# Three real products instead of four for the spectral multiplication, with the last seven frequencies of four units packed together

## The chip, the cores and the metric

The kernel runs on one core of one Trainium2 chip. The metric is device time in microseconds (us): the time of one execution as the device reports it. TensorE (PE) multiplies matrices into PSUM (8 banks of 128 partitions x 512 fp32), VectorE (DVE), ScalarE (ACT) and GpSimd (POOL) work elementwise, SyncE (SP) issues the DMAs.

## What is computed

For each of 4 batch entries, 6272 steps and 256 channels: a gated recurrence, then three projections of its result, a circular convolution over time of the middle one with a given filter, a product of the three, and an output projection.

```python
sig = 1.0 / (1.0 + np.exp(-f_logit))
f = lower_bound + (1.0 - lower_bound) * sig
h = f[:, t] * h + (1.0 - f[:, t]) * x[:, t]        # for each t, giving y
...
proj = y @ w_proj                                  # three blocks of 256: x1, x2, x3
X2 = np.fft.rfft(x2, n=S, axis=1)                  # S = 6272
H = np.fft.rfft(filter_fft, n=S, axis=0)
x2_conv = np.fft.irfft(X2 * H, n=S, axis=1)
out = (x1 * x2_conv * x3) @ w_out
```

The line that the change touches is `X2 * H`: a product of complex numbers for each frequency and channel.

## The kernel before, in words

**Transform.** 6272 is 128 x 49. The Fourier transform is done as two small transforms by matmul: one over 128 (table `D1`), one over 49 (table `FT`, with its inverse in `VA` and `VB`), with the channels as further columns. After the first transform a channel pair holds 64 columns `k`; the second turns the 49 residues into 49 frequencies with a real and an imaginary part: 98 rows (`TB`). Channels are worked in 16 *units* (`NU`) of 8 channel pairs (`UE`); four units (`NA`) form a group whose first transforms lie in the tile `A` at the same time.

**Setup** (`prepare`). It builds the tables (`iotas`, `args0`, `args1`: DVE makes arguments, ACT takes the sine; then table pieces on DVE and POOL), loads the filter, rotates it (`rot`, line 637), and transforms it unit by unit: `FF1` (line 661), copies `afs`, `FF2` (line 679), a copy `hw`, and a store to the DRAM tiles `H`. The spectrum of the filter is stored with some rows twice, so that a load can bring both (real, imaginary) and (imaginary, real) orders to the 98 rows. `last` (line 697) does the column `k = 0` apart. In between, the recurrence of batch entry 0 runs.

**Recurrence** (`hgrn`, 13 chunks of 512 steps): loads, `sig` on ACT (line 337), `u` on POOL (339), `su` transposes on PE (351), `f` on ACT or DVE (364, 366), `scan` on DVE (372), `wrap`, a copy of the first 3072 steps behind the last (303 on POOL, 291 on ACT, or a DMA).

**Each batch entry** then goes through
- `P` (line 725): the middle projection, 98 matmuls, with copies `x2` into the tile `X2`;
- for each group of four units: `F1` (737) and the copy `A` for each unit; `mini` (753) with the product `zm` (761) for the column `k = 0`; then for each unit `H` (load of the filter's spectrum), `F2` (795, eight matmuls of 64 contracted rows, two side by side), the products, `I2` (835, sixteen matmuls back) and the copy `Th`;
- `gate`: `x13` (line 400), copies `xs`, and `z` = x1 * x3, on DVE straight from PSUM (422) or on POOL (431);
- `phase_o`: `I1` (869), `y` on DVE (875), `proj` (887), copy `o`, store.

`y` needs every `z` and `I1` needs every `Th`, so the gate and all units of a batch entry come before its output stage; the recurrence of the next entry is woven into both.

**The products.** A unit's spectrum stands in two PSUM banks (one for each channel of the pairs). For each bank the product with the filter has 2 x 8 x 63 = 1008 elements on 98 rows: (real, imaginary) times two arrangements of the filter. Either DVE does it straight from PSUM (`MUL`, line 816), or ACT or DVE copies the bank to SBUF and POOL multiplies (`pm`, 825). `I2` sums the two halves with `VA` and `VB`.

**Order.** Every operation is numbered as the code is read. `ORDER` is a string with three characters for each operation: its number, its engine and its PSUM bank. `Plan.emit` issues the operations in that order, so it fixes the order on every engine and who does what. The numbers in `op(...)` such as `{"PE": 0.43}` are a planner's costs; they do not act when the kernel runs. PSUM is taken in pairs of banks by most operations, so there are four pairs.

Of the kernel before, what the change touches and what calls it, by code (L numbers as in the profile page):

```python
# [9 lines left out]
F32 = mybir.dt.float32  # L10
# [11 lines left out]
S = 6272  # L22
# [3 lines left out]
TB = 98  # L26
CH = 512
# [14 lines left out]
HP = 128  # L42
HT = 64
# [3 lines left out]
PW = 116  # L47
# [17 lines left out]
class Plan:  # L65

    ROWS = ("su", "F2", "mini", "I1", "FF2", "last")
# [73 lines left out]
    "J4XGluJyYJ2BGsUGgSG1QJ3YGwEGhKGmYHQgJ5WJ6PG5AMrgHGSGtYMsgGkYJ9VJ7uGxYHHCJ+RGusJ8YGpWJ/FHMSGqGG3oGvYG+UG6YHZgKABHIW"
    "HNKG4YGyQHJGHAsHKSGzAG2YHigKBYG7WHLCHCsHBYKCQG/YG8GHORHRTHDYHrgHPJKDVHTDHVrHSYKHXKEAHUYKITKJHKFtKMSHWYMtAHEQKKrKGY"
    "KOKHaWKLYHFAMuYH+gH0UHcuHXSH1EH4QHeuHdYHYCHjUHbYHkYH5AHlsHfYIHgH2WMWYHgSH3GHnsHmYHsQHhCH6WHuoHoYIQgHpUHtYH7GMiYH/S"
    "HwoHvYHqEH8WKNQIBCIIUH9OHxYIZgIDqIRRICYIKEHyWITBKPoIEYKRUHzGIMsKQYKSTIiQIAYKTEIsgILYIFWIjAINYKUrKWVKVYKXTIGGKYNMXQ"
    "KZDIJYIVpI1gISYIaWIUYMYAMbUIeGMZIIWYIOSM3gMcEM4gKbXIPCMdMKaYI+gIXQKdHImSIYAIcuIbYMegMjUIfYInCIkQMkMIdYIoWIlAKcTMlM"
    "KgSMaYJHgIpGItQKerKiCIqUMnWIvoKfYIxAKhTNDgMoGIyYIgRIrMNEgIwYM5AMpOKlQI2UIhBKjrMvWIuYKnAI3YI6sKkYMzSM6YMwGKmQNPgI4E"
    "MxOKqRI7YNQgM0CIzUKsBM1KM7WI5YI0ENFAKrVKooKvTKttKpYM8GM/QNGYKuYKxDJIUM9ONbgNAAI8SNcgJMENBIKwXJKEK0WI9CJLYI/UKyvK2G"
    "K1RJBsKzYNHSK3BNRAK5WJDsJCYJAYK4YNLQNICNlgK7OJEYJFUNMANSYNmgNJKK6WJGEK+XNdANNINKgK/VNTTLAHJJYNeYK8uNXQNUDLBtK9YLDX"
    "NvgNYANVLLEWLCYMygLFHLISNwgLJVLKCNOgLNXJNYLGuLLFNfSNZILHYLPHNiUNgCLOWN6gNnANhKLMYN5gJOQNWgNjENoYLQuRtSJPANkMRuXLRY"
    "RvCLSQRwHLXSLTINxANpUMmYNsWLYKNqENyYLUQODgNtGOEgNrMLZSLVANuOLcULaCLWgNzQLdMRyWN0ALhSR0GN1IN2UN7ALmWONgN3ELiKOOgLeQ"  # L150
    "N8YLbgOFAM+gN4MLjSMqgLfALnOLrULkCOGYN9QLsMOAWN+ALoSOXgOBGN/IOYgM2gOHULpCNagOCOLwQOPAOKSLxILtWUwgOLCOQYLlgOIEOMKLyQ"
    "LuGOJML1SLzAORWL2KL0gRzROSGLqgL6UOZANCAOTOOUSOaYR1BU8gL7MU9gObWL3QOcGOVCOdOOWKOeUL4AL8WVJgVIgOfMUxgMEQL9GOgMLvgL/S"
# [825 lines left out]
```

## Time and profile before

| | |
|---|---|
| device time, median of 3 runs | 460.54 us (460.45 to 461.36) |
| profiled execution: device time | 459.27 us |
| profiled execution: span, first to last instruction | 457.5 us |
| mean granted clock of TensorE | 0.998 |
| `P` of the four entries starts at | 73.8, 169.9, 271.3, 368.9 us |
| last instruction | 457.5 us |

The span leaves out 1.8 us of the profiled execution's time, and that execution lies 1.3 us below the median of the runs. The stages are read by time: setup with the first recurrence to about 74 us, then for each entry a stage `P` of some 11 us, a stage of units and gate, and a stage of output with the rest of the next recurrence; the last entry has no next recurrence. A PE instruction's record reaches to a modelled end, so a busy PE is not a PE at full rate. For the rate one takes pieces of the chain of waits in which matmuls of one kind follow each other, and divides the time by their number.

### The profile page before, as it was taken

How to read it: one execution, taken by the hardware profiler on the slowest of the kernel's cores; microseconds unless marked ns; L12 is line 12 of the kernel's file. 1: busy time of each engine (PE TensorE's matmuls, PEld its weight loads, DVE VectorE, ACT ScalarE, POOL GpSimd, SP SyncE). 2: the span in 40 equal slices, each digit the busy share in tenths (PEclk: the TensorE clock that was granted, in tenths of full speed). 3: DMA queues.
4: the chain of work that ended last, by engine and by line, in shares of the span. 5: the costliest groups of instructions: out<-in, count | busy, mean ns of one | idle time of the engine just before them, and what ended most of it. 6: DMA issues, size and time to landing. Idle time of an engine off the chain costs nothing.

```text
span 457.5 us, 14613 instructions
## 1 busy us (share of the span) xinstructions
PE 443.7 (97%) x6009; PEld 346.2 (76%) x6009; DVE 408.9 (89%) x461; ACT 399.3 (87%) x550; POOL 300.9 (66%) x274
## 2 busy tenths in 40 slices
PE   8998999999999999999999999999999999999995
PEld 6876777767766889777668889767768897677784
DVE  7599996799999993999999986999999977999873
ACT  5989998889999989989998979999989868988563
POOL 4489892289899425778996616989896405976400
PEclk9999999999999999999999999999999999999999
DMA  8999999776979997477779995487969930575176
GB/s 323 407 366 333 357 356 347 284 262 203 313 259 298 326 339 299 179 250 246 241 272 287 350 315 240 142 288 297 308 205 308 351 124 18 192 238 179 48 294 271
DMA packets 46451, 122.59 MB, mean 268 GB/s; under 512 B 4528, under 2 KB 9648, under 8 KB 46384
## 3 DMA queue, kind: packets, MB, share of 16 engines
q1 hardware_dynamic: 46384, 121.65, 75.4%
q8 instruction: 47, 0.77, 0.7%
q14 instruction: 20, 0.16, 0.1%
HBM read 86.12 MB, written 31.98 MB: 258 GB/s over the span
## 4 chain that ended last, share of the span: by engine, by line
PE 70%; DVE 15%; ACT 8%; issue 4%; POOL 2%; DVEq 0%; ACTq 0%; POOLq 0%
PE PS L400 15%; PE PS L725 9%; PE PS L835 8%; PE PS L887 8%; PE PS L351 7%; DVE HA L372 6%; PE PS L737 6%; PE PS L795 6%; DVE ys L875 4%; PE PS L637 3%; PE PS L869 3%; PE PS L661 3%; ACT fTs L364 2%; ACT HA L291 2%; PE PS L603 2%
## 5 line engine op out<-in xcount | busy, mean ns | idle before, releaser
L339 POOL TENSOR_TENSOR XT<-XT,FL 128x1024 f32<-128x1024 f32 (+1 forms) x49 | 110.0, 2247 | 52.1 <-ACT FL L337 28.9
L372 DVE TENSOR_TENSOR_SCAN HA<-fTs,HA,PS 128x512 f16<-128x512 f32 (+1 forms) x96 | 113.2, 1203 | 1.1 <-ACT fTs L364 0.2
L400 PE MATMUL PS<-HA,W 128*128 128x490 f16 (+1 forms) x416 | 102.7, 367 | 1.0 <-DVE HA L372 0.4
L825 POOL TENSOR_TENSOR PP<-HA,Hu 98x1008 f16<-98x1008 f16 x38 | 79.7, 2104 | 5.1 <-ACT HA L291 2.7
L291 ACT CAST HA<-PS 128x1024 f16<-128x1024 f32 (+1 forms) x96 | 78.2, 837 | 5.3 <-PE PS L737 2.9
L431 POOL TENSOR_TENSOR zt<-gx 128x490 f16<-128x490 f32 (+1 forms) x43 | 52.1, 1217 | 45.0 <-DVE ys L875 16.7
L816 DVE TENSOR_TENSOR PP<-PS,Hu 98x1008 f16<-98x1008 f32 x58 | 68.1, 1200 | 0.0
L875 DVE TENSOR_TENSOR ys<-PS,zt 128x1024 fp32r<-128x1024 f32 (+1 forms) x52 | 58.9, 1152 | 7.8 <-PE PS L869 4.7
L887 PE MATMUL PS<-Wo,ys 128*128 128x256 f32 x392 | 58.2, 294 | 1.6 <-DVE ys L875 1.5
L364 ACT ACTIVATE fTs<-PS,cc 128x512 f32<-128x512 f32 (+1 forms) x83 | 54.8, 675 | 5.1 <-PE PS L351 4.3
L400 PEld LDWEIGHTS <-W 128*128 128x128 f16 x416 | 34.6, 97 | 30.4 <-issue 6.8
L835 PEld LDWEIGHTS <-PP 98*128 98x128 f16 x1024 | 49.9, 97 | 9.7 <-issue 1.6
L835 PE MATMUL PS<-VV,PP 98*128 98x98 f16 x1024 | 55.9, 206 | 0.3
L887 PEld LDWEIGHTS PS<-Wo,ys 128*128 128x128 f32 x392 | 49.7, 188 | 6.6 <-DVE ys L875 2.9
L291 ACT CAST Th<-PS 128x784 f16<-128x784 f32 x59 | 48.3, 821 | 6.6 <-PE PS L835 4.6
L293 ACT ACTIVATE gx<-PS 128x490 f32<-128x490 f32 (+1 forms) x84 | 48.3, 584 | 2.5 <-PE PS L400 1.5
L337 ACT ACTIVATE FL<-FL 128x1024 f32<-128x1024 f32 (+1 forms) x49 | 49.4, 1010 | 0.0
L725 PE MATMUL PS<-W,HA 128*128 128x256 f16 x392 | 44.6, 273 | 0.2
L351 PEld LDWEIGHTS PS<-iden,FL 64*128 64x128 f32 x736 | 31.2, 138 | 16.8 <-DVE HA L372 2.9
L725 PEld LDWEIGHTS <-HA 128*128 128x128 f16 x392 | 42.9, 142 | 1.3 <-DVE HA L372 0.3
L351 PE MATMUL PS<-iden,FL 64*128 64x64 f32 x736 | 42.2, 231 | 1.6 <-DVE HA L372 0.8
L291 ACT CAST X<-PS 128x1024 f16<-128x1024 f32 (+1 forms) x31 | 32.6, 1092 | 10.3 <-PE PS L725 9.0
(130 smaller groups left out, 745.6 us busy)
## 6 DMA issues: line engine op xcount, KB each, us to landing
FL<-in_f_logit_dram SPq DMA_DIRECT2D x45, 512.0 KB, 5.5
XT<-in_x_dram SPq DMA_DIRECT2D x45, 512.0 KB, 6.4
Hu<-H SPq DMA_DIRECT2D x39, 512.0 KB, 4.8
out_dram<-osb SPq DMA_DIRECT2D x22, 512.0 KB, 4.6
out_dram<-PP SPq DMA_DIRECT2D x16, 512.0 KB, 5.3
Hx<-H SPq DMA_DIRECT2D x13, 512.0 KB, 4.4
out_dram<-HA SPq DMA_DIRECT2D x10, 512.0 KB, 5.5
X<-in_moe_filter_fft_dram SPq DMA_DIRECT2D x9, 512.0 KB, 7.2
```

Source lines behind the costliest of these rows:

```text
L291: nc.scalar.copy(dst, src)
L339: op("u", {"POOL": 0.1 + 0.553 * nb}, lambda e, xt=xt, ft=ft: nc.gpsimd.tensor_tensor(xt, xt, ft, op=AOP.mult), r=[("ft", k)], w=[("xt", k)])
L351: nc.tensor.transpose(bank(pb)[:, at[p] + j:at[p] + hn:nb], src[ps, j, cols], iden[ps, ps])
L364: nc.scalar.activation(fT, sT, AF.Identity, scale=by, bias=1.0)
L372: nc.vector.tensor_tensor_scan(h, fT, bank(pb)[:, 512 - hn:512 + hn], init, op0=AOP.mult, op1=AOP.add),
L400: nc.tensor.matmul(PS[:, p, 0:n], W13[:, kh, js], HA[:, HB[kh] + t0:HB[kh] + t0 + n], start=(kh == 0), stop=(kh == 1))
L725: nc.tensor.matmul(pp[:, r - r0, :], column(HB[kh], q_of(r)), W2[:, kh, :], start=(kh == 0), stop=(kh == 1))
L816: nc.vector.tensor_tensor(pr, px.unsqueeze(1).broadcast_to([TB, 2, UE, 63]), hh, op=AOP.mult)
L825: nc.gpsimd.tensor_tensor(pr, spec[:, o, :, 1:64].unsqueeze(1).broadcast_to([TB, 2, UE, 63]), hh, op=AOP.mult)
L835: nc.tensor.matmul(PS[:, ib + o, pr * TB:(pr + 1) * TB], PP[:TB, k, o, n, 2 * pr:2 * pr + 2, :], v[:TB], start=(n == 0), stop=(n == 1))
L875: nc.vector.tensor_tensor(late["ys"][:, yk, :, 0:rn * 128], PS[:, cb:cb + 2, 0:rn * 128], late["zt"][:].rearrange("p k r m -> p k (r m)") ...
L887: nc.tensor.matmul(po[:, i, :], late["ys"][:, yk, kh, i * 128:(i + 1) * 128], Wo[:, kh, :], start=(kh == 0), stop=(kh == 1))
```

## The change

The complex product is done with three real products: with X = a + ib and the table rows for a, b and a + b, one multiplies three rows by three rows of the filter's spectrum and lets the inverse table do the sums. Rows per frequency go from 2 to 3, elements per row from 2 to 1. 49 x 3 = 147 rows do not fit 128 partitions, so 42 frequencies (`QM`; 126 rows, `KM`) are done unit by unit, and the last 7 (`QL`; 21 rows) of four units go into four blocks of 32 partitions of one tile. `F2` writes 126 rows with the same eight matmuls; its products have 8 x 63 = 504 elements per bank instead of 1008. New for each group of four units: `FL` (32 matmuls with 32 weight columns each), `slot`, and `pl` on DVE (1008 elements). `mini` has ten matmuls instead of four and `zm` two products. `I2` keeps sixteen matmuls: one of each pair takes the unit's own rows, the other the packed ones with a table that is zero outside the unit's block.

In the setup: `FFL` (8 operations of 8 matmuls) and `hwl` (4 copies) make the packed filter spectrum, which stays in SBUF (`HL`); `last` has 20 matmuls; `args1` and the tables grow; the store of the spectrum is one DMA of 126 rows for each two units instead of two, and a load brings 126 rows of 1024 numbers instead of 128 rows of 2048. `X2` has a pitch of 114 instead of 116. The order is new: 2460 entries instead of 2410.

```diff
-PW = 116
+PW = 114
...
-    FT = konst.tile([128, 2, 2, 128], F16, name="FT")
+    FT = konst.tile([128, 2, 2, 160], F16, name="FT")
+    VM = konst.tile([128, TB], F16, name="VM")
+    VL = konst.tile([128, NA, TB], F16, name="VL")
...
-                        nc.tensor.matmul(PS[:, pb + e2, :], FTr[rows, r, 0:M], af[rows, r],
+                        nc.tensor.matmul(PS[:KM, pb + e2, :], FTm[rows, r], af[rows, r],
...
+                def rest(e, pb, u=u):
+                    for j in (u % NA - 1, u % NA):
+                        for r in range(2):
+                            for e2 in range(2):
+                                rows = slice(64 * e2, 64 * e2 + 64)
+                                at = 96 + 128 * r - 32 * j
+                                nc.tensor.matmul(PS[:, pb + e2, :], FTl[rows, at:at + 128],
+                                                 afs[j % 2][rows, r], start=(j == 0 and r == 0),
+                                                 stop=(j == NA - 1 and r == 1))
+                more = u % NA == NA - 1
+                hl = op("FFL", {"PE": 0.9}, rest, r=[("af", j, h) for j in range(2) for h in range(2)] + FTu,
+                        w=[("FF2L", u // NA)], **(dict(src=fl) if more else dict(take=2)))
...
+                    op("hwl", either(1024), lambda e, pb, q=u // NA: copy(e, HL[q], PS[:, pb:pb + 2], HS),
+                       r=[("FF2L", u // NA)], w=[("HL", u // NA)], src=fl)
...
+    def rest(b, q):
+        k = count["l"] % NP
+        count["l"] += 1
+        def mm(e, xb):
+            for o in range(2):
+                ks = slice(32 * o, 32 * o + 32)
+                for r in range(2):
+                    for j in range(NA):
+                        for e2 in range(2):
+                            rows = slice(64 * e2, 64 * e2 + 64)
+                            nc.tensor.matmul(
+                                PS[32 * j:32 * j + 32, xb + e2, :].rearrange("p (i k) -> p i k", k=64)[:, :, ks],
+                                FT[rows, o, r, 128:160], A[rows, j * UE:(j + 1) * UE, r, ks],
+                                start=(r == 0), stop=(r == 1))
+        fl = op("FL", {"PE": 0.65}, mm, r=[t for i in range(NA) for t in At(i) + Ax(i)] + ["FT0", "FT1"], take=2)
...
+        op("pl", {"DVE": 1.11}, lambda e, xb: nc.vector.tensor_tensor(
+            PP[:, k, 1, :, :, 1:64], blocks(PS[:, xb:xb + 2]), blocks(HL[q]), op=AOP.mult),
+           r=[("HL", q)], w=[("PL", k)], src=fl)
...
-            Hv(h)[:HP].rearrange("p a e k -> p a (e k)"), turned(H[u // 2][u % 2])),
+            Hv(h)[:KM].rearrange("p e k -> p (e k)"), H[u // 2][0:KM, u % 2]),
...
-                            PS[:, xb + e2, :].rearrange("p (i k) -> p i k", k=64)[:, :, ks],
-                            FT[rows, o, r, :], A[rows, ka:ka + UE, r, ks],
+                            PS[:KM, xb + e2, :].rearrange("p (i k) -> p i k", k=64)[:, :, ks],
+                            FT[rows, o, r, 0:KM], A[rows, ka:ka + UE, r, ks],
...
-                    nc.vector.tensor_tensor(
-                        pr, px.unsqueeze(1).broadcast_to([TB, 2, UE, 63]), hh, op=AOP.mult)
+                    nc.vector.tensor_tensor(pr, px, hh, op=AOP.mult)
...
-                    nc.gpsimd.tensor_tensor(
-                        pr, spec[:, o, :, 1:64].unsqueeze(1).broadcast_to([TB, 2, UE, 63]), hh,
-                        op=AOP.mult)
+                    nc.gpsimd.tensor_tensor(pr, spec[:, o, :, 1:64], hh, op=AOP.mult)
...
-                    for n, v in enumerate((VA, VB)):
-                        nc.tensor.matmul(PS[:, ib + o, pr * TB:(pr + 1) * TB],
-                                         PP[:TB, k, o, n, 2 * pr:2 * pr + 2, :], v[:TB],
+                    for n, (a, v) in enumerate(((PP[:KM, k, 0, o], VM[:KM]), (PP[:, kl, 1, o], VL[:, u % NA]))):
+                        nc.tensor.matmul(PS[:, ib + o, pr * TB:(pr + 1) * TB], a[:, 2 * pr:2 * pr + 2, :], v,
                                          start=(n == 0), stop=(n == 1))
```

What the two orders, read entry by entry, give to each engine (operations of a kind, before and after):

| | before | after |
|---|---|---|
| products: DVE straight from PSUM / copy by ACT / copy by DVE (both copies then POOL) | 85 / 41 / 2 | 74 / 45 / 9 |
| `A`: ACT / DVE | 55 / 9 | 48 / 16 |
| `Th`: ACT / DVE | 59 / 5 | 55 / 9 |
| `xs` copies: ACT / DVE | 118 / 29 | 116 / 38 |
| `z`: DVE from PSUM / POOL | 61 / 43 | 54 / 50 |
| `wrap`: ACT / POOL / DMA | 3 / 18 / 27 | 12 / 14 / 22 |
| `afs`: ACT / DVE | 24 / 8 | 20 / 12 |
| new on PE | | 16 `FL`, 8 `FFL` |

On SP, one half of the first chunk's loads of the recurrence now stands ahead of the filter's loads, and ACT's first operation is that chunk's `sig`.

369 lines of the change are left out of this document (210 added, 159 removed).

## Prediction

> **What bounds the kernel now.** I read the page's first part, the windows by stage, the chain of waits for the rate of each kind of matmul, and the groups of instructions by shape. First the page and the windows (window in us, length, then busy time of PE, PEld, DVE, ACT, POOL with instruction counts, clock, DMA share, GB/s):
>
> ```profile
> PE 443.7 (97%) x6009; PEld 346.2 (76%) x6009; DVE 408.9 (89%) x461; ACT 399.3 (87%) x550; POOL 300.9 (66%) x274
> ```
> ```profile
> 0.00:22.00 22.00, 20.62 (x117) 16.92 (x117) 15.21 (x46) 16.49 (x16) 10.52 (x28) 1.00 0.93 364
> 22.00:74.00 52.00, 49.30 (x617) 37.95 (x615) 48.63 (x54) 49.68 (x73) 42.20 (x46) 1.00 0.97 348
> ...
> 85.00:144.00 59.00, 57.66 (x843) 40.25 (x841) 57.12 (x64) 55.75 (x82) 51.17 (x42) 1.00 0.78 255
> 144.00:170.00 26.00, 24.96 (x426) 21.01 (x426) 25.70 (x26) 23.44 (x33) 13.27 (x8) 1.00 0.94 332
> ...
> 382.00:430.00 48.00, 47.91 (x630) 34.40 (x629) 46.02 (x56) 40.91 (x62) 36.21 (x37) 1.00 0.45 146
> ```
>
> PE looks full everywhere, but DVE and ACT are nearly full too: in the units-and-gate stage of entry 0 (85 to 144) DVE 57.12 of 59 us, in the output stage (144 to 170) 25.70 of 26. What PE really needs comes from rates. Pieces of the chain between 12 and 100 us (start, length, what):
>
> ```profile
> 26.88 1.03 PE PS L351 x32
> ...
> 29.25 1.24 PE PS L679 x8
> ...
> 67.03 1.14 PE PS L661 x8
> ...
> 84.64 1.65 PE PS L400 x8
> ...
> 92.35 0.11 PE PS L753 x4
> 92.47 0.44 PE PS L795 x8
> ...
> 94.70 0.75 PE PS L835 x16
> 95.45 0.45 PE PS L737 x8
> ```
>
> So one matmul takes 0.206 us (`x13`), 0.047 (`I2`), 0.055 (`F2`: 0.11 for a side-by-side pair), 0.056 (`F1`), 0.032 (transposes), 0.143 (`FF1`) and 0.155 (`FF2`). Now the matmuls of the stage 85 to 144, and two rows of 382 to 430 (where there are no transposes, and the others are the same 256, 128 and 128):
>
> ```profile
> L400 PE MATMUL PS<-HA,W 128*128 128x490 f16 x83 | 21.0, 370 | 0.2 <-ACT Th L291 0.2
> L835 PE MATMUL PS<-VV,PP 98*128 98x98 f16 x256 | 14.0, 206 | 0.0
> L795 PE MATMUL PS<-HA,FT 64*128 64x256 f16 x128 | 9.5, 271 | 0.0
> L737 PE MATMUL PS<-D,X 128*128 128x128 f16 x128 | 9.5, 219 | 0.5 <-DVE HA L296 0.2 <-ACT HA L291 0.2
> L351 PE MATMUL PS<-iden,FL 64*128 64x64 f32 x112 | 6.3, 232 | 0.0
> L351 PE MATMUL PS<-iden,XT 64*128 64x64 f32 x112 | 5.9, 223 | 0.1
> ```
> ```profile
> L400 PE MATMUL PS<-HA,W 128*128 128x490 f16 x84 | 20.7, 370 | 0.0
> ...
> L400 PE MATMUL PS<-HA,W 128*128 128x392 f16 x8 | 1.5, 328 | 0.0
> ```
>
> Stage 85 to 144: 91 x 0.206 + 256 x 0.047 + 128 x 0.055 + 128 x 0.056 + 224 x 0.032 + 0.45 for `mini` = 52.6 of 59 us: 0.89. (Eight of the 91 are shorter; the sum is an upper one.) Stage 382 to 430: 92 x 0.206 + 12.0 + 7.0 + 7.2 + 0.45 + about 1 for eight projection matmuls = 46.6 of 48 us: 0.97. So with the next recurrence woven in, DVE (0.97) and ACT (0.94) limit, and PE has some 6 us to spare; in the last entry PE itself limits. The clock is 1.00 throughout and plays no part.
>
> **The change part by part.**
>
> *Elementwise work of the entries.* The rows (mean ns of one):
>
> ```profile
> L825 POOL TENSOR_TENSOR PP<-HA,Hu 98x1008 f16<-98x1008 f16 x38 | 79.7, 2104 | 5.1 <-ACT HA L291 2.7 <-DVE zp L761 1.3 <-PE PS L835 0.9
> L816 DVE TENSOR_TENSOR PP<-PS,Hu 98x1008 f16<-98x1008 f32 x58 | 68.1, 1200 | 0.0
> ...
> L291 ACT CAST HA<-PS 128x1024 f16<-128x1024 f32 x55 | 55.2, 1020 | 3.6 <-PE PS L737 2.9 <-issue 0.2
> ...
> L431 POOL TENSOR_TENSOR zt<-gx 128x490 f16<-128x490 f32 x40 | 49.1, 1232 | 43.1 <-DVE ys L875 16.7 <-ACT gx L293 11.4 <-ACT gx L291 9.2
> L291 ACT CAST Th<-PS 128x784 f16<-128x784 f32 x59 | 48.3, 821 | 6.6 <-PE PS L835 4.6 <-DVE gx L296 1.2
> ...
> L422 DVE TENSOR_TENSOR zt<-PS,gx 128x490 f16<-128x490 f32 x56 | 36.4, 656 | 1.1 <-ACT gx L293 0.8
> ...
> L291 ACT CAST HA<-PS 98x512 f16<-98x512 f32 x41 | 23.1, 591 | 1.8 <-PE PS L795 0.9 <-PE PS L753 0.4
> ...
> L296 DVE CAST HA<-PS 128x1024 f16<-128x1024 f32 x9 | 10.9, 1220 | 1.5 <-PE PS L737 1.1 <-POOL PP L825 0.4
> ...
> L296 DVE CAST Th<-PS 128x784 f16<-128x784 f32 x5 | 4.8, 967 | 0.1
> ...
> L296 DVE CAST HA<-PS 98x512 f16<-98x512 f32 x2 | 1.4, 676 | 0.0
> ```
>
> A product of 504 elements on DVE isn't in the trace; the 490-element product of `z`, 0.656 us, is the nearest row, so 0.66 (half of 1.20 would be 0.60). DVE before: 85 x 1.20 = 102.0 (the 58 of the row and 27 that read `Hx`). After: 74 x 0.66 + 16 `pl` x 1.20 = 68.0. Removed: 34.0. But the order gives DVE more copies: `A` 7 x 1.22 + `Th` 4 x 0.97 + copies ahead of POOL 7 x 0.68 + nine `xs` at 0.66 less seven `z` at 0.66 + one `x2` of 1024 elements at 1.22 = 19.7. Net -14.3 us, **-3.6 for each entry**. ACT: -7 x 1.02 - 4 x 0.82 + 4 copies at some 0.6 - 3 others at 0.6 to 1.1, plus five more `wrap` copies at 0.6: about -7, -1.8 for each entry. POOL: 43 x 2.10 = 90.4 (38 and 5 with `Hx`) against 54 x 1.1 (half of 2.10 to the 1.23 of the 490-element row) = 59, and 7 more `z` and 16 small `slot`: -18 in all. POOL is not full (66%); shorter products shorten a unit's way to `I2`, nothing else. The loads of the spectrum carry half as much, but no wait in the stages ends on them, so I count this at nothing.
>
> *PE in the entries.* `F2` and `I2` keep their matmuls and columns: nothing. `FL`: 32 matmuls of 256 columns, eight tiles side by side. Column tiles are not in the trace. If all eight run together as `F2`'s two do: 4 x 0.11 = 0.44 us. If matmuls cannot follow each other closer than the 0.032 of the transposes: 1.0. If only pairs run together: 32 x 0.055 = 1.76. I take 0.75, between the first two, since the starts of a side-by-side pair are what `F2` already shows. `mini` has six matmuls more at 0.03: +0.2. So 4 x 0.95 = **+3.8 us for each entry** (2.6 to 7.8).
>
> The Trainium skill, page "TensorE: Matmul & The Clock Gate", section "Part 3: Packing small matmuls — row/col tiling", states that packed tiles take one matmul's time and about 4 ns for each further tile. By it `FL` would be an estimated 4 x (0.11 + 0.03) = 0.55 us, and the sum 0.8 us less for each entry; no run here shows column tiles yet.
>
> *Where these meet.* Stage 85 to 144: PE 52.6 + 3.8 = 56.4. At the 0.97 that the last entry shows feasible this takes 58.1 us, so the 3.6 that DVE gives can shorten the stage by 0.9 at most unless transposes move behind it. I take **-1 for each of three entries: -3**. Last entry: 46.6 + 3.8 = 50.4, at 0.97 52.0 instead of 48: +4; DVE there is at 46.02 of 48 and gets 3.6 free, which may let PE run a little denser: **+3.5**. The tail behind 430 does not change.
>
> *Setup.* DVE before 22 us: `args1` gets about 20 more column operations and the tables some more:
>
> ```profile
> L293 ACT ACTIVATE Hu<-PS 128x1024 f16<-128x1024 f32 x6 | 6.0, 1024 | 0.6 <-PE PS L679 0.5
> ...
> L545 DVE SCALAR_TENSOR_TENSOR cols<-cols 128x1 f32<-128x1 f32 x1 | 0.2, 160 | 0.0
> ```
>
> 20 x 0.16 = 3.2, and some 2 for wider tables: 15.2 + 5.2 = 20.4 of 22 us busy, so its waits for the rotated filter no longer fit; and half a chunk, 0.5 MB at 364 GB/s = 1.4 us, is loaded ahead of the filter. `FF1` starts later by 1.5 (0 to 3); behind it stand all `afs` and so `FF2`. From 22 to 74: ACT +4 `hwl` x 1.02 and four `wrap`, less one `sig` and the moved copies: +4; DVE +2.8 (four `afs`, one `hw`, two fewer `f`). Both are at 0.94 to 0.96 there, so half of 6.8, 3.4, less 1 for gate work done early: +2.5. PE: eight `FFL` at 1.24 us (eight matmuls of `FF2`) = 9.9, and `FF1` 128 x 0.143 + `FF2` 64 x 0.155 + 392 transposes x 0.032 = 40.8 leave it 11 of 52 us: hidden just about, but each group holds one of four PSUM pairs from its first `FFL` to `hwl`: +1. The stores are halved; DMA share is 0.97 there, yet the waits there end on DMA only for the filter's first loads: nothing. Setup: **+5** (2 to 10).
>
> Sum: 5 - 3 + 3.5 = **+5.5 us**. Against the profiled execution's own 459.27 that is 464.8; the median of the runs shown lies 1.27 above it, so I forecast **466.0** for the median.
>
> **The rivals.**
>
> *DVE decides (ends faster).* Mechanism: between 85 and 170 us DVE is busy 82.8 of 85 us and every other engine less. If `FL` costs 0.44 (PE +2.6) and the order moves half of the stage's transposes (3.6 us) into the output stage, the whole 3.6 that DVE gives comes off each of the three entries: -10. With the last entry at +1 and setup at +2.5: -7, so 453.5. It decides from the point where `FL` costs less than about 0.6 us. For it: DVE at 0.97 to 0.99 in both stages. Against it: ACT at 0.94 gives only 1.8.
>
> *No change.* The same terms in between (entries -2.5 each, last +2.5, setup +5) give 460.5.
>
> *Setup decides.* `FFL` and its held PSUM pair are not hidden: +9.9 instead of +1 on top of the start: setup +10 to 14, in all 471 to 475. Against: the 11 us that PE has there.
>
> *Column tiles do not run together.* `FL` at 1.76: +16 in all, PE over 0.97 in every stage: 466 + 14 = 480. For: nothing in the trace shows more than two tiles together.
>
> *Weight loads become visible.* These rows are the loads of `F2` and of the transposes:
>
> ```profile
> L351 PEld LDWEIGHTS PS<-iden,FL 64*128 64x128 f32 x736 | 31.2, 138 | 16.8 <-DVE HA L372 2.9 <-issue 2.9 <-ACT gx L291 1.5
> ...
> L795 PEld LDWEIGHTS <-FT 64*128 64x128 f16 x512 | 22.0, 96 | 9.9 <-issue 6.5
> ```
>
> `F2`'s weights go from 128 to 126 columns. If its loads took the 138 ns of the transposes' and stood open: 42 ns x 512 = 21 us, 487. Against: the transposes have those loads and still follow each other at 32 ns, and each pair of `F2` streams 110 ns over them. The Trainium skill, same page, section "Weight-path perf modes — Fast Weight Load (FWL) and DoubleRow", says that the fast load needs exactly 128 weights and a type other than fp32, which speaks against this change; the trace agrees in that fp32 loads are longer (138 against 96 ns).
>
> **How the numbers follow.** Forecast (461.5 to 470): 0.40. DVE decides (448 to 459.5): 0.33. No change: 0.08. Setup: 0.09. Column tiles: 0.06. Weight loads: 0.04. A measurement of this kernel tells about 0.2% (0.9 us) from no change. Faster by more: 0.33; within: 0.08; slower: 0.59. The range leaves out the two dearest rivals and the far third of the faster one: 451 to 477. The likeliest case alone is 461.5 to 470.
>
> **What would show it.** Right or wrong are: `FL`'s length in the chain (0.44, 0.75, 1.76); the 504-element product on DVE (0.66) and on POOL (1.1); the start of the first `P` (73.8 before; 79 by the forecast); the length from the first to the second `P` (96 before; 95, and 92.5 if DVE decides); the last entry's stage from `P`'s end to its last `I2` (48 before; 51.5). The forecast is wrong if `FL` lies outside 0.44 to 1.0, if setup grows by less than 2, or if the three middle entries each lose or gain over 3 us.

## The result, and the profile after

The changed kernel takes 483.67 us (median of 4 runs, 483.28 to 485.88) against 460.95 us for the kernel before on the same chip: a ratio of 1.049 (95% interval 1.044 to 1.054). It is slower by 22.7 us, where 5.5 were forecast, and lies outside the range. The profiled execution took 483.28 us with a span of 481.5 us.

The first part of the page of the changed kernel (busy time, share of the span, instructions):

```profile
span 481.5 us, 16035 instructions
...
PE 466.5 (97%) x6693; PEld 365.6 (76%) x6693; DVE 405.4 (84%) x535; ACT 401.8 (83%) x550; POOL 281.1 (58%) x304
```

PE is busy 22.8 us longer than before (443.7), and the span grew by 24.0 us. (Both spans are of the profiled executions; that of the kernel before was 1.7 us faster than its median here and that of the changed kernel 0.4, so the stage differences below add up to 24.0 and not to 22.7.) PE's idle time, span less busy, is 13.8 us before and 15.0 after. DVE's busy time fell by 3.5 us, POOL's by 19.8, and neither shows in the time. The same in the windows of the stages (setup, then units and gate, output, and the last entry's units and gate):

```profile
24.00:81.50 57.50, 54.74 (x654) 41.77 (x652) 50.16 (x52) 52.39 (x73) 41.00 (x46) 1.00 0.85 297
...
93.00:154.00 61.00, 60.04 (x949) 44.86 (x947) 51.68 (x73) 52.92 (x74) 41.61 (x48) 1.00 0.47 150
154.00:182.00 28.00, 27.53 (x470) 22.34 (x468) 27.96 (x26) 26.17 (x40) 17.68 (x10) 1.00 0.88 310
...
399.00:453.00 54.00, 54.00 (x796) 39.27 (x795) 43.04 (x66) 41.20 (x60) 30.16 (x43) 1.00 0.25 81
```

In the units-and-gate stage DVE went from 57.12 of 59 us to 51.68 of 61: the relief arrived, and the stage became longer. Only in the output stage is DVE still full. The stages by the starts of `P` (us):

| | first `P` | entry 0 | entry 1 | entry 2 | entry 3 to the end |
|---|---|---|---|---|---|
| before | 73.7 | 96.1 | 100.4 | 98.6 | 88.7 |
| after | 85.5 | 99.2 | 103.6 | 102.6 | 90.6 |
| difference | +11.8 | +3.1 | +3.2 | +4.0 | +1.9 |

The sum is 24.0. (These are first matmuls on PE's timeline; in the chain of waits of the kernel before the first `P` begins at 73.8 and entry 2's at 271.3, after its first rows at 270.2.) Within an entry, from `P`'s end to the last `I2` takes 2.4, 4.8, 3.9 and 2.3 us longer; the output stages differ by -1.6 to +0.3.

What was added, in the groups by shape of the changed kernel (the new products, then `FL`, `FFL`, `mini`, and the weight load of `F2`):

```profile
L908 DVE TENSOR_TENSOR PP<-PS,Hx 126x504 f16<-126x504 f32 x40 | 26.0, 674 | 2.8 <-PE PS L887 2.2 <-ACT HA L295 0.4
...
L852 DVE TENSOR_TENSOR PP<-PS,Hu 128x1008 f16<-128x1008 f32 x16 | 19.2, 1200 | 0.4 <-PE PS L844 0.4
...
L916 POOL TENSOR_TENSOR PP<-HA,Hf 126x504 f16<-126x504 f16 x30 | 34.0, 1143 | 6.4 <-ACT HA L295 2.7 <-issue 2.4 <-DVE HA L300 1.1
...
L844 PE MATMUL PS<-HA,FT 64*32 64x256 f16 x512 | 10.0, 270 | 0.0
...
L734 PE MATMUL PS<-afs,Hf 64*128 64x512 f32 x32 | 5.6, 426 | 0.0
L734 PE MATMUL PS<-Hx,Hf 64*128 64x512 f32 x32 | 5.0, 388 | 0.0
L813 PE MATMUL PS<-HA,FT 64*126 64x64 f16 x32 | 4.7, 288 | 0.1
L818 PE MATMUL PS<-HA,FT 64*32 64x16 f16 x128 | 3.5, 196 | 0.0
...
L887 PEld LDWEIGHTS <-FT 64*126 64x126 f16 x512 | 27.0, 132 | 9.0 <-issue 7.0
```

And one `mini`, `FL` and the `F2` behind it on PE's timeline (start, length, operation):

```profile
202.75 0.30 PE L813 MATMUL PS<-HA,FT 64*126 64x64 f16 x2
202.98 0.22 PE L818 MATMUL PS<-HA,FT 64*32 64x16 f16 x8
203.02 0.62 PE L844 MATMUL PS<-HA,FT 64*32 64x256 f16 x32
203.56 0.65 PE L887 MATMUL PS<-HA,FT 64*126 64x256 f16 x8
```

`FL` holds PE for 0.54 us here, and 0.57 in the mean of the sixteen. The 270 ns in its group are modelled ends of overlapping matmuls, so what counts is the distance from start to start.

PE's whole timeline can be added up in this way, from each start to the next one, so that a wait counts with the matmul ahead of it. Behind the first `P`, `FL` takes 9.1 us and `mini` 5.0 instead of 1.8: 12.3 us more. All other matmuls there together take 381.9 us, against 382.0 before. Ahead of the first `P`, `FFL` takes 8.8 us, `last` 0.7 more and the matmuls without a use that fill PE's time before `FF1`, with the waits behind them, 2.4 more; the rest together is the same to 0.1 us. So the 24 us are PE's new work, some 21.8 us, and 2.4 us at the start, and nothing that DVE and POOL gave back made the rest of PE's work any shorter.

In the setup DVE's arguments take 9.6 us in one piece (9.05 to 18.6; before 3.96), and the copies of the rotated filter stand behind them on DVE; `FF1` starts at 25.3 instead of 22.2. `FFL` stands in the chain of waits (start, length, what):

```profile
30.26 1.13 PE PS L734 x8
...
44.84 0.99 PE PS L734 x8
...
60.60 1.12 PE PS L734 x8
65.45 0.97 PE PS L734 x6
74.72 1.12 PE PS L734 x8
78.96 1.11 PE PS L734 x7
```

At its end PE stands still inside the first `P`, until two copies on ACT let go (timeline):

```profile
84.61 3.06 ACT L297 ACTIVATE X<-PS 126x512 f16<-126x512 f32 x2
...
85.48 1.04 PE L786 MATMUL PS<-W,HA 128*128 128x256 f16 x8
...
87.72 1.47 PE L786 MATMUL PS<-W,HA 128*128 128x256 f16 x12 [1.20 <-ACT X L297]
```

These are the copies of the column `k = 0`: before it was one of 1.4 us.

### The profile page after: what moved, and what is told of

It is laid out like the page before. It is cut to its first block, busy times and chain, and to the rows that moved or that the text cites. A ratio compares the mean times of both kernels' runs of the same rounds, so it can differ in the third digit from the quotient of the medians.

```text
span 481.5 us, 16035 instructions
## 1 busy us (share of the span) xinstructions
PE 466.5 (97%) x6693; PEld 365.6 (76%) x6693; DVE 405.4 (84%) x535; ACT 401.8 (83%) x550; POOL 281.1 (58%) x304
## 4 chain that ended last, share of the span: by engine, by line
PE 76%; DVE 15%; issue 3%; ACT 3%; POOL 2%; DVEq 0%; POOLq 0%; ACTq 0%
PE PS L404 16%; PE PS L924 9%; PE PS L786 9%; PE PS L355 8%; PE PS L976 7%; PE PS L887 7%; DVE HA L376 6%; PE PS L798 6%; DVE ys L964 5%; PE PS L958 3%; PE PS L697 3%; PE PS L844 2%; PE PS L639 1%; PE PS L715 1%; PE PS L734 1%
## 5 line engine op out<-in xcount | busy, mean ns | idle before, releaser
L404 PE MATMUL PS<-HA,W 128*128 128x490 f16 (+1 forms) x416 | 105.1, 367 | 0.7 <-DVE HA L300 0.6
L435 POOL TENSOR_TENSOR zt<-gx 128x490 f16<-128x490 f32 (+1 forms) x50 | 60.7, 1218 | 66.4 <-DVE gx L300 22.8
L295 ACT CAST HA<-PS 128x1024 f16<-128x1024 f32 (+1 forms) x93 | 72.3, 810 | 14.1 <-PE PS L887 7.3
L924 PEld LDWEIGHTS <-PP 126*128 126x128 f16 (+1 forms) x1024 | 51.2, 98 | 8.9 <-issue 1.5
L924 PE MATMUL PS<-VM,PP 126*128 126x98 f16 x512 | 54.3, 208 | 0.0
L924 PE MATMUL PS<-VL,PP 128*128 128x98 f16 x512 | 54.1, 207 | 0.0
L404 PEld LDWEIGHTS <-W 128*128 128x128 f16 x416 | 33.4, 97 | 26.4 <-issue 6.2
L297 ACT ACTIVATE gx<-PS 128x490 f32<-128x490 f32 (+1 forms) x82 | 46.8, 579 | 8.0 <-PE PS L404 6.1
L295 ACT CAST Th<-PS 128x784 f16<-128x784 f32 x55 | 44.9, 820 | 7.0 <-PE PS L924 5.6
L355 PE MATMUL PS<-iden,XT 64*128 64x64 f32 x736 | 39.4, 223 | 0.2 <-POOL XT L343 0.2
```

The source lines that it names most:

```text
L295: nc.scalar.copy(dst, src)
L355: nc.tensor.transpose(bank(pb)[:, at[p] + j:at[p] + hn:nb], src[ps, j, cols], iden[ps, ps])
L404: nc.tensor.matmul(PS[:, p, 0:n], W13[:, kh, js], HA[:, HB[kh] + t0:HB[kh] + t0 + n], start=(kh == 0), stop=(kh == 1))
L435: nc.gpsimd.tensor_tensor(zd(), xs(0), xs(1), op=AOP.mult)
L924: nc.tensor.matmul(PS[:, ib + o, pr * TB:(pr + 1) * TB], a[:, 2 * pr:2 * pr + 2, :], v, start=(n == 0), stop=(n == 1))
```

## The experiments

Two theories stood against each other. A (in the expectations also "PE theory"): PE sets the time, and the PE work that the change adds is the loss. B ("order theory"): the new order is the loss (waits made by its sequence), and the work would have fitted. The "DVE theory" is the forecast's: DVE sets the time where the next recurrence is woven in. Spans, PE busy and idle come from each run's profiled execution; the kernel before beside the runs took 460.6 to 461.2 us.

| run | time us | ratio (95%) | PE busy | PE idle | DVE busy |
|---|---|---|---|---|---|
| before | 460.95 | 1 | 443.7 | 13.8 | 408.9 |
| after | 483.67 | 1.044 to 1.054 | 466.5 | 15.0 | 405.4 |
| e1_pe_added | 468.63 | 1.016 to 1.019 | 453.7 | 13.3 | 410.5 |
| e2_half_products | 459.57 | 0.994 to 0.999 | 442.8 | 14.5 | 371.3 |
| e3_half_and_pe | 467.50 | 1.013 to 1.017 | 453.5 | 12.3 | 371.1 |
| e4_tile_form | 471.71 | 1.023 to 1.026 | 455.6 | 14.6 | 409.1 |
| e18_same_form | 463.26 | 1.003 to 1.008 | 447.1 | 14.0 | 410.1 |
| e11_setup_work_old_order | 466.18 | 1.009 to 1.016 | 450.6 | 13.3 | 410.2 |
| e12_fewer_tile_changes | 469.30 | 1.015 to 1.022 | 445.6 | 21.7 | 410.3 |
| e17_all_work_old_order | 495.71 | 1.067 to 1.079 | 464.6 | 29.5 | 393.5 |
| e9_old_work_new_order | 529.31 | 1.146 to 1.154 | 460.8 | 65.2 | 421.4 |
| e5_thin_rest | 481.13 | 1.042 to 1.046 | 461.4 | 17.4 | 404.8 |
| e6_no_ffl | 484.51 | 1.046 to 1.053 | 461.4 | 21.6 | 405.7 |
| e7_small_out | 482.27 | 1.044 to 1.049 | 467.0 | 13.7 | 405.6 |
| e8_short_args | 482.56 | 1.045 to 1.049 | 465.7 | 15.1 | 402.5 |
| e10_all_thin | 477.35 | 1.033 to 1.039 | 456.1 | 19.5 | 401.6 |

**One engine at a time, in the old order.** e1 adds twelve matmuls ahead of each `mini`; e2 halves the products; e3 does both.

```diff
+            for o, r in ((0, 0), (0, 1), (1, 0)):
+                for i in range(2):
+                    for e2 in range(2):
+                        nc.tensor.matmul(PS[:, pb + e2, 0:256], FT[rows, o, r, :],
+                                         A[rows, 8 * i:8 * i + 8, r, 0:32], start=True, stop=True)
...
-                        pr, px.unsqueeze(1).broadcast_to([TB, 2, UE, 63]), hh, op=AOP.mult)
+                    nc.vector.tensor_tensor(pr[:, 0], px, hh[:, 0], op=AOP.mult)
```

> The kernel before, with twelve more matmuls of 256 columns (64 contracted rows, in side-by-side pairs) ahead of each group's mini; their results are overwritten by mini itself, so nothing else changes. At F2's 0.055 us each this is 0.66 us of PE for a group, 2.6 us for an entry, 10.6 us in all; the order of everything stays. PE theory (PE sets the time in every entry, what it lacks to its dense rate are changes of tile form that nobody can fill): +9 to +11 us. DVE theory (the forecast's: PE has some 6 us to spare in a stage of 59 as long as the next recurrence is woven in): +2 to +4 us, nearly all in the last entry. Order theory (the longer time is due to the new order, not to the work): +4 us at most.

> The kernel before, with the products of one half only: 504 elements instead of 1008 on DVE and on POOL, and I2 reads that half twice, so PE has the same work and the result lacks the imaginary part's share. DVE gets 85 x 0.53 = 45 us less, POOL 43 x 0.96 = 41 us less, and the order stays. PE theory: 0 to -4 us. DVE theory: -8 to -14 us, since DVE is at 0.97 to 0.99 in the entries' stages and three of four entries gain more than 3 us each. Order theory says nothing here.

> Both edits of the kernel before at once: products of one half, and twelve more matmuls for each group. This is the entries' part of the change (less on DVE and POOL, more on PE) in the old order, without the setup's part. PE theory: +7 to +11 us, as in the first. DVE theory: -6 to +1. Order theory: the same as DVE theory, with the rest of the entries' 12 us coming from the new order.

e1 costs 8.0 us for 10.0 us of PE busy time: 0.8 us for each us. That is a little under A's 9 to 11 and far over the 2 to 4 of the DVE theory. Its entries take 98.6, 103.2, 100.9 and 90.4 us, nearly those of the changed kernel. Its page:

```profile
PE 453.7 (97%) x6201; PEld 357.0 (76%) x6201; DVE 410.5 (88%) x461; ACT 399.9 (86%) x550; POOL 300.5 (64%) x274
```

e2 takes 37.6 us off DVE and 39.5 off POOL and gains 1.7 us by its ratio. Its page and its DVE products:

```profile
PE 442.8 (97%) x6009; PEld 346.7 (76%) x6009; DVE 371.3 (81%) x461; ACT 398.2 (87%) x550; POOL 261.4 (57%) x274
```
```profile
L816 DVE TENSOR_TENSOR PP<-PS,Hu 98x504 f16<-98x504 f32 x58 | 38.1, 676 | 5.4 <-ACT Th L291 2.1 <-PE PS L832 1.1 <-ACT HA L291 1.0
```

In e3 the relief pays for 1 us of what the matmuls cost. In the old order PE sets the time of the entries, and relief on DVE and POOL is worth nearly nothing: the rival "DVE decides" falls here.

**Why PE is full at 0.89.** The rates of the prediction left 6 us of 59 free. e4 puts one tiny matmul of 64 rows at the head of each of the 48 operations of `P`; e18 one of 128 rows at the same places.

First e4's line, then e18's, each at the head of the function that `P` issues.

```diff
+                nc.tensor.matmul(pp[:, 0, 0:32], FT[0:64, 0, 0, :], ID[0:64, 0, 0:32], start=True, stop=True)
```
```diff
+                nc.tensor.matmul(pp[:, 0, 0:32], D1[:], ID[:, 0, 0:32], start=True, stop=True)
```

> The kernel before, with one tiny matmul (64 contracted rows, 32 columns) at the head of each of the 48 operations of P; it is overwritten by the next matmul. Two changes of tile form for each, 128 rows to 64 and back. In the trace of before, x13 to F2 takes 0.30 us from start to start against 0.21 from x13 to x13, and the way back 0.20 against 0.05, so 0.24 for a round trip. PE theory: the stage P, where PE is dense, gets 12 x 0.24 = 2.9 us longer in each entry, 10 to 12 us in all. If the larger spacing in the trace is only waiting for other engines: 12 x 0.03 = 0.4 us for an entry, under 2 us in all.

> The kernel before with one tiny matmul of 128 rows and 32 columns at the start of each of the 48 P operations, where e4 had one of 64 rows (+11.3 us). If e4's cost is the change of the tile's form, this costs 48 x 0.03 to 0.05 = 1.5 to 2.5 us, 462 to 463.5; if any extra matmul there costs that much, 470 or more.

48 of them cost 11.1 us with 64 rows and 2.7 us with 128. Timeline of e4, then of e18:

```profile
74.59 0.19 PE L723 MATMUL PS<-ID,FT 64*128 64x32 f16 x1
74.71 0.66 PE L726 MATMUL PS<-W,HA 128*128 128x256 f16 x4
```
```profile
74.30 0.18 PE L723 MATMUL PS<-ID,D 128*128 128x32 f16 x1
74.33 1.28 PE L726 MATMUL PS<-W,HA 128*128 128x256 f16 x8
```

From the tiny matmul to the next start it is 119 ns (median of 48) in e4 and 28 in e18; from a `P` matmul to the tiny one 205 (median of 42) and 109. So a change between 128 and 64 rows costs some 0.09 us in each direction. The kernel before makes 256 of them, the changed one 264. If all cost what these do, that is an estimated 24 us of PE time that no rate of one kind shows. In the stage 85 to 144 there are 40: an estimated 3.7 us more than the 52.6 counted, 56.3 of 59. The Trainium skill, page "TensorEngine Tiling (Array Packing)", section "Key Properties", says that changing the tiling mode drains TensorE. These runs agree in that a change costs time, and give the 0.09 us; a drain as such no trace shows.

e12 used that: fourteen entries of the list's 2410 pulled ahead on PE (five `su`, two `F2`, two `x13`, two `F1`, one `FF1`, `FF2` and `I2`), so that forms change 228 times. The first line of `ORDER` that differs:

```diff
...
-    "CYMEiAEQWEXYCQUE4gEROCWCB8gAIACRME5gAKAESOCTSENABsYEYUCUCEOIEcWFCgCeSEdGCSYCZYEZMFDgCgQEjYAHAEeOCfCChACaSEaMEuACnQ"
+    "CYMEiAEQWEXYCQUE4gEROCWCB8gAIACRME5gAKAESOCTSENABsYEYUCUCEOIEcWFCgCeSEdGCSYCZYEZMFDgCgQEjYAHAEeOCfCChACaSEaMEuAEkW"
...
```

> The kernel before with fourteen of its 2410 list entries pulled forward on PE, so that operations with 64 rows stand together and PE changes between 128 and 64 rows 228 times instead of 256. By 0.235 us for each round trip this saves 14 x 0.235 = 3.3 us of PE time: 457.5 us if PE's changes of form are on the path, 460 to 463 if the pulled operations wait for their inputs instead.

It is slower by 8.6 us, beyond both expectations. PE's idle time rose by 8 us, which fits operations that now wait for their inputs, and others behind them. What fewer changes would save can't be read from it, since the places moved too.

**The setup.** e11 repeats `FF2` of every second unit in the kernel before. In the changed kernel, e6 leaves out fourteen of the sixteen `FFL` matmuls of each group, but not the operations; e7 writes the last column in the order of its memory; e8 leaves out 24 column operations.

```diff
-                for r in range(2):
+                for r in range(2) if not u % 2 else (0, 1, 0, 1, 0, 1):
```
```diff
-                    for j in (u % NA - 1, u % NA):
-                        for r in range(2):
+                    if u % NA < NA - 1:
+                        return
...
```
```diff
-            copy(e, Hm[:KM], PS[:KM, pb:pb + 2, 0:2 * NEP].rearrange("p e (k i) -> p e k i", k=2), HS)
+            copy(e, xv[:KM, :, Q:Q + 4].rearrange("p i (e k) -> p i e k", e=2),
+                 PS[:KM, pb:pb + 2, 0:2 * NEP].rearrange("p e (k i) -> p i e k", k=2), HS)
```
```diff
-            ts(js, in0=prow[:], scalar1=32.0, scalar2=None, op0=AOP.is_ge)
...
+            dve.memset(cols[:, 9:23], 1.0)
```

> The kernel before with FF2 of every second unit repeated three times, in its old order: 64 matmuls of 512 columns more in the setup, the PE time of the eight FFL (about 9 us), without their PSUM pair and without the new order. If PE work in the setup is what moved the first P by 11.7 us, the first P starts at 80 to 83 and the time is 467 to 470 us; if the held PSUM pair or the order did, the first P starts at 74 to 76 and the time is 461 to 463.

> The changed kernel with two matmuls for each group's FFL instead of sixteen; the packed filter spectrum is then wrong. FFL took 8.8 us of PE from start to start in after, now some 1.5 to 2. PE theory: -6 to -7 us, all of it ahead of the first P (85.5 us after). DVE theory or order theory: -2 at most, with the setup still held by DVE and ACT.

> The changed kernel with the copy of the column k = 0 of the filter written pair by pair in the order of memory (channel pair, then part), as before the change, instead of part by part with a step of 228 bytes. In after the two copies take 2.49 and 1.11 us on ACT, 3.06 together, and P stands still for 2.2 us behind them. If the step of the destination sets the time: some 1.2 us together, P resumes 2 us earlier, -1.5 to -2 us in all. If it is the number of elements or the PSUM side: no change.

> The changed kernel without 24 of the column operations in args1 (their columns are set to 1, so the tables VM and VL are wrong). DVE's args1 gets 3.2 us shorter. In after FF1 starts at 25.3 us against 22.2 before, and the chain runs through args1, the copies fr behind it on DVE, rot and the last copy. If that chain sets the start: FF1 2.5 to 3 us earlier, and -2 to -3 us in all. If the half chunk loaded ahead of the filter sets it: FF1 no more than 1 us earlier, under -1 in all.

e11 moves the first `P` to 80.7 (+7.1) and the time by 5.5 us, for 7.0 us of PE from start to start: so in the old order PE's free time in the setup was not there. e7 gains 1.4 us, about what the stall suggests. e8 gains 1.1, not the 2 to 3 that the argument columns alone would give: `FF1` comes only 0.9 us earlier, at 24.4, and the chain of waits then begins with the load of the filter. e6 speaks against theory A: with `FFL` at 3.1 us instead of 8.8 the first `P` still starts at 84.9 and nothing is gained; `FF1` and `FF2` get 3.6 us longer from start to start, by waits. Its window of the setup:

```profile
24.00:81.50 57.50, 50.52 (x605) 37.56 (x604) 50.49 (x54) 53.28 (x75) 42.17 (x48) 1.00 0.85 295
```

PE is now idle 7 of 57.5 us, and no engine is full (ACT, the busiest, 53.28). The list still reserves a PSUM pair for `FFL` and keeps every other operation in its place.

**Removing the rest, and the orders exchanged.** e5 thins `FL` and `mini` in the changed kernel (2 matmuls of 512 columns instead of 32, 4 instead of 10); e10 joins e5, e6, e7 and e8. e9 issues the work of the kernel before in the new list (the new operations dropped); its diff shows the first line of `ORDER`.

```diff
-            for o in range(2):
-                ks = slice(32 * o, 32 * o + 32)
-                for r in range(2):
-                    for j in range(NA):
...
+            for e2 in range(2):
+                rows = slice(64 * e2, 64 * e2 + 64)
+                nc.tensor.matmul(PS[:, xb + e2, :].rearrange("p (i k) -> p i k", k=64),
+                                 FT[rows, 0, 0, 0:128], A[rows, 0:UE, 0, :], start=True, stop=True)
```
```diff
...
-    "AAYA+gBBgAMYABIAZVACIBFgAaSBMgAtRBPgAmXAqSBTgAdTBIgA9YANIAcSBagAbUAoQAvVAwXA/WBCABDQBAGBGSBEIBogAOABdgBQAAPIBNQBWg"
+    "AAYDwgA+gAMYABIAZSACIBFgAmRBIgAoVBMgAlXAkUBBgAsVBTgA9YANIAcXBWgAjTAwXAhRAuSAeUADgDyAA/VBPgBagBGQBANBdgBJAAPIApVBog"
...
```

> The changed kernel with FL and the second part of mini thinned: FL is two matmuls of 512 columns (64 rows by 128 columns, the form that F2 has) instead of 32 column tiles, mini four matmuls in the same form; the packed rows then hold one unit's values only, so the result is wrong in the last seven frequencies. FL took 0.57 us and mini 0.31 in the trace of after; now some 0.22 and 0.10, and the change to the narrow form and back goes: about 0.5 us for a group, 8 us in all. PE theory: -6 to -8 us. Order theory: -2 at most, since the order and what waits on it stay.

> The changed kernel with nearly all that was added taken out of the engines' time at once, in its new order: FL and mini thinned, two FFL matmuls left for each group, the copy of the last column written contiguously, 24 column operations of the argument tables left out (the packed rows and the tables are wrong in it). Each of these alone gave 0 to 2.5 us. Theory A (added work on engines that are critical together): relief adds up to more than the single ones, 465 to 472 us. Theory B (the new order): about the sum of the single ones, 2.5 + 0 + 1.4 + 1.1 = 5 us, so 477 to 479.

> The kernel before, with its own operations, issued in the order, on the engines and in the PSUM banks that the changed kernel's list gives them (the new operations are dropped from that list). Theory A, the added PE work is what costs: this kernel has none of it, so it stays within 3 us of before, 458 to 464 us. Theory B, the new order itself costs (waits that its sequence makes, whatever the work): 470 us or more, and the P starts lie near those of the changed kernel (85, 185, 288, 391). The old products are longer on DVE and POOL, and the new list gives DVE more of the copies, so under A a few us on the slow side are possible; between 464 and 470 both have a part.

e5 gains 2.5 us for 5.1 us of PE, e10 6.3 us for 10.4: 0.5 to 0.6 for each us, less than the 0.8 that adding costs. Both are nearer to what theory B expected (at most 2, and 477 to 479) than to A's 6 to 8 and 465 to 472. In part the edits are weaker than meant: the thinned `FL` still takes 0.42 us from start to start and `mini` 0.16, where 0.22 and 0.10 were expected, so 4.9 us of PE went and not 8. And e10's first `P` starts at 83.9, only 1.6 us earlier, so in the setup hardly anything of what was taken out comes back.

e9 is far slower than either kernel. That is over the bound of theory B, but B also wanted its `P` to start near those of the changed kernel, and they start at 82.9, 192.9, 307.5 and 423.1. Its page:

```profile
PE 460.8 (88%) x6009; PEld 352.3 (67%) x6009; DVE 421.4 (80%) x475; ACT 399.5 (76%) x545; POOL 328.4 (62%) x288
```

No engine is full. The list was run with products of 1.2 us on DVE and 2.1 on POOL where it had stood beside products of 0.67 and 1.14: that the list is good only for the lengths of its own operations would explain it, but is not shown, and e9 tells nothing of what the list costs with them. The opposite exchange is e17, all of the change's work (by stand-ins) in the old list: the edits of e3 and e11, the copy of the last column twice, and

```diff
+            nc.vector.tensor_scalar(PS[:TB, pb:pb + 2, 0:504], in0=PS[:TB, pb:pb + 2, 0:504],
+                                    scalar1=1.0, scalar2=None, op0=AOP.mult)
             nc.vector.tensor_tensor(zp[:TB, q % 2], px, Hm[:TB, :, :, :, es], op=AOP.mult)
...
+            for _ in range(24):
+                ts(sgn, in0=sgn, scalar1=1.0, scalar2=None, op0=AOP.mult)
```

> The kernel before in its old order with stand-ins for all that the change adds and takes away: 504-element products (I2 reads one half twice), 12 matmuls ahead of each mini (+10.6 us of PE, as in e1), FF2 of every second unit three times (+9 us, as in e11), a pass of 1008 elements on DVE in each zm (as pl), 24 column operations more in args1, and the copy of the last column twice. Theory A (the added work costs, in whatever order): 467.5 of e3, 5.5 of e11, 2 for args1 and the copy, 2 to 5 for the DVE passes: 477 to 480 us, most of the way to 483.67. Theory B (the new order is the loss): the relief on DVE and POOL pays for part of it, 470 to 474.

It takes 495.71 us, 12 more than the changed kernel and far over both expectations. Its first `P` starts at 85.8, as the changed kernel's (85.5): in the old order, too, the setup's work delays it as much. But the entries don't settle the choice between A and B. The stand-in for `pl` stands ahead of the product of `mini`, which the real `pl` does not, and behind the first `P` e17 takes 16.7 us more than e3 and has the same added matmuls; PE's idle time is 29.5 us against 12.3. So most of what e17 loses in the entries is this pass of 1.2 us on DVE, sixteen times, in a place for which PE waits:

```profile
L769 DVE TENSOR_SCALAR PS<-PS 98x1008 f32<-98x1008 f32 x16 | 19.5, 1217 | 16.2 <-PE PS L761 14.3 <-ACT fTs L364 1.1 <-ACT gx L293 0.8
```

Without it, what e3 and e11 cost by themselves (6.9 and 5.5 us) makes 12.4 us of the 22.7.

**Lists fitted anew.** e13 to e16 rearrange the lists of before, after, e10 and e2, by a replay of the list with the start-to-start times of the trace: 93 to 109 operations on PE stand elsewhere, and 89 to 143 copies change between ACT and DVE. The first line of e13's `ORDER`:

```diff
...
-    "AAYA+gBBgAMYABIAZVACIBFgAaSBMgAtRBPgAmXAqSBTgAdTBIgA9YANIAcSBagAbUAoQAvVAwXA/WBCABDQBAGBGSBEIBogAOABdgBQAAPIBNQBWg"
+    "AAYAtRAaSAdTBFgBBgAmXAwXAoQABIACIBCAAqSAcSAMYANIA+gAPIA9YBGSAZVBDQBEAAvVA/WBAGBMgBPgAOAASIATYBTgBHKBIgBJYBagBQABNQ"
...
```

> The kernel before, all its work unchanged, with its list rearranged: 93 of 770 operations on PE, 48 on DVE and 108 on ACT stand elsewhere, and 89 copies change between ACT and DVE, chosen by replaying the list with the start-to-start times of the trace (that replay gives 458 us for the list as it is, 452 for the new one). If a list can still be fitted better, 453 to 456 us; if the replay misses what makes the old list good, 460 to 470, as with e12.

> The changed kernel, all its work unchanged, with its list rearranged in the same way (102 operations on PE, 71 on DVE, 128 on ACT; 128 copies change sides; the replay gives 477 for its own list, 469 for the new one). Theory A (added work costs): it gains about what e13 gains, 474 to 477 us, and the distance between the two fitted kernels stays at 17 us or more. Theory B (the changed kernel's list is a bad fit): it gains 15 us or more and comes near 460 to 466.

> The changed kernel with FL and mini thinned, two FFL matmuls for each group, the contiguous copy and the short argument tables, as in e10 (477.35), but with the list fitted to that work. Theory A: the time that the fixed list hid comes back, 463 to 468 us. Theory B, or a list that cannot be fitted further: within 3 us of e10, 474 to 480.

> The kernel before with 504-element products as in e2 (I2 reads one half twice; 459.57), with the list fitted to them. If DVE and POOL held the time and only the old list hid their relief (the rival DVE decides), 442 to 446 us, 8 to 10 below e13; if PE holds it, within 3 us of e13, 450 to 454.

Measured: 473.38 (ratio 1.023 to 1.032), 491.45 (1.065 to 1.070), 482.85 (1.045 to 1.052) and 468.04 (1.012 to 1.021). All four are slower than the lists they came from and lie above every time expected of them; the replay lacks something that the old lists have room for, and what it is wasn't found. No version here beats the kernel before, except e2, which computes something else. Among the four, the added work costs 18.1 us (e14 less e13), thinning it returns 8.6 (e14 less e15), and halving the products alone gains 5.3 (e13 less e16). But each has a list of its own, and a new list alone cost 8.6 us in e12 and 12.6 in e13, so these differences are no prices of the work.

## Why the prediction was wrong, step by step

- **The free time of PE in the entries** is the step that failed: "PE has some 6 us to spare". It had at most an estimated 2.7: the changes of form, 3.7 us in that stage, were in no rate. And not even this was used, since the rest of PE's work took as long as before. So the three middle entries didn't gain 1 us each but lost 3.1, 3.2 and 4.0, about the 3.1 us of PE that each one got; e1 repeats this with PE work alone (+2.5, +2.7, +2.3). The sum had -3 here, and the trace +10.3. A loss of over 3 us in each of them is a sign of being wrong that the prediction itself named.
- **"DVE and ACT limit"** failed with it. DVE busy 57.12 of 59 was read as a bound; e2 took 37.6 us off DVE for 1.7 us. No run relieved ACT alone.
- **`FL`** was taken at 0.75 and measured 0.57, between the bounds. The Trainium skill's estimate (page "TensorE: Matmul & The Clock Gate", "Part 3: Packing small matmuls — row/col tiling") of 0.55 was nearer. `mini` was taken at +0.2, and it is 0.31 instead of 0.11: right. So 3.1 us of PE for each entry instead of 3.8; the size was no fault.
- **The last entry**: +3.5 forecast, +1.9 measured; from `P`'s end to its last `I2` 50.7 us, where 51.5 were forecast. This was the one stage where PE was named as the limit.
- **The setup**: +5 forecast, +11.8 measured. `FF1` came 3.1 later instead of 1.5, just beyond the bounds. `FFL`, "hidden just about", was priced well (1.1 us each, forecast 1.24) but not hidden: from start to start PE spends all of its 8.8 us more, and e11 moves the first `P` by 7.1 us with such work. Again 42 changes of form (an estimated 3.9 us) were missing from the 40.8 counted. The strided copy of the last column, 3.06 us, wasn't seen at all: 1.4 us by e7. That `FFL` alone holds the first `P` is not shown, since e6 takes most of it out and gains nothing.
- **The products** came out as priced: 0.67 us on DVE (0.66), 1.14 on POOL (1.1).
- **Rivals.** "Setup decides" had the right place and size for its part (+10 to 14), though its total of 471 to 475 was short of the measured one. "Column tiles not together" and "weight loads visible" fell. `F2`'s loads did become longer, 132 ns against 96, and yet `F2`'s 512 matmuls take 34.7 us from start to start against 34.1. The longer loads agree with the Trainium skill's rule on the fast load (page "TensorE: Matmul & The Clock Gate", "Weight-path perf modes — Fast Weight Load (FWL) and DoubleRow"). "DVE decides" had a chance of 0.33; e2's 1.7 us and e3 speak against it.
- **Two sums of the rivals** don't come out: the terms of "DVE decides" (-10, +1, +2.5) give -6.5 and 454.0 instead of 453.5, and +16 for the column tiles gives 482 instead of 480. Neither bears on the failure.

Shown is that added PE work costs 0.8 us for each us in the old order (e1, e11), and that in the changed kernel PE's added work, from start to start, and 2.4 us of waits ahead of `FF1` are the whole difference. At 0.8 the 22.8 us of PE busy time explain some 18 of the 22.7 us. Taking such work out of the new order returned 0.5 to 0.6 (e5, e10), and nothing in e6. So the entries' part of the loss is PE's work. How much of the setup's 11.8 us is `FFL`, and how much the new order with its reserved PSUM pair and fixed places, stays open: these were argued, not tried apart.

## What to carry to other kernels

Work out an engine's need from rates only after adding what lies between the kinds: here the 64-row and 128-row matmuls in turn cost PE an estimated 24 us that no kind's rate holds, and the "free" tenth of PE wasn't free. Busy shares near 1 on two engines don't tell which one limits; taking work off one and adding some to the other, in a run each, does (e2 and e1). In a kernel with a written-out order, price added work at nearly full cost and removed work at half or less; new orders made here by a replay did not do better.

## What the runs showed of the hardware

- A change between 128-row and 64-row matmuls at the head of `P`'s operations takes about 0.09 us of PE in each direction (e4 against e18).
- Eight column tiles of 64 x 32 follow each other at a median of 3 ns from start to start: 32 matmuls of 256 columns in 0.57 us.
- A copy of 512 elements per partition on ACT whose 2-byte results lie 228 bytes apart took 2.49 us, and 1.03 us in e7, where four results lie together.
- Fourteen operations of 2410 moved cost 8.6 us (e12), with no work added.
